# A gated recurrence feeding a two-layer block on one core: log sums, transposes and totals on 64-row tiles, and a longer list of steps

## The chip, the cores and the metric

The kernel runs on one core of one Trainium2 chip. The metric is the device time of one launch in microseconds, lower is better. The median of three runs before the change is 605.38 us (605.31 to 607.55).

## The reference

Two stages are chained. The first is a gated linear recurrence over 768 positions, for 4 batches and 8 heads of width 48; the second applies two weight matrices with an activation between them to the resulting 3072 rows of 384.

```python
f = 1.0 / (1.0 + np.exp(-f_logit))
for t in range(S):
    state = f[:, :, t, :, None] * state + einsum('bhd,bhe->bhde', k[:, :, t], v[:, :, t])
    y[:, :, t] = einsum('bhd,bhde->bhe', q[:, :, t], state)
x = y.transpose(0, 2, 1, 3).reshape(B * S, H * D)      # (3072, 384)
h = x @ w_in                                           # (3072, 2048)
sp = np.maximum(h, 0.0) + np.log1p(np.exp(-np.abs(h)))
out = (h * erf(sp)) @ w_out                            # (3072, 384)
```

All tensors of the recurrence are float32. The two weight matrices arrive as 8-byte numbers, which the kernel itself turns into float32 (a "rounding" of seven steps for each of 16 pieces, one step on ACT and six on VectorE).

## The kernel before

The rows are cut into 24 chunks of 128 positions, and each chunk into two halves of 64. A block is two chunks (256 rows), so there are 12 blocks.

For each chunk g the recurrence does the following; the short names are those of the list of steps.

- f, q, k, v: loads on SP's queue. `load_f` (L229) brings the gate logits as one DMA of 192 KB into `lt`, with the positions on the partitions. cl, ex, ln: clamp, exp and log of `lt`, for -log of the gate.
- d, `log_sums` (L396): running sums of the logs within each half, as one product of a 128x128 triangular matrix `tri` with `lt`, 384 columns, into one PSUM bank. e, `decays` (L400, L401): two exps out of that bank, into `dp` and `kd`. qd, kd (L414, L421): q and k times them, on VectorE.
- tq, tk, `transposes` (L437): four transposes of 128x128 each for q and for k into PSUM; aq, ak (L443, L449 or L451): copies of them to SBUF, on ACT or VectorE.
- ds, `state_products` (L499), and sc, `scores` (L510): products on 64x64 tiles into the two banks of `sc_all`. m and s: masks on the scores (L535 to L544). to, ta, `sum_totals` (L518): for chunks below 6 the total decay of each half, taken out of `dp` by products with columns of the identity; tt sends the totals of later chunks by small DMAs.
- st, `add_state` (L473 to L476), and sp, `copy_state` (L481): the running state of VectorE and its copies into `sv` on POOL (GpSimd), two per half chunk. v with four digits, L249, and w, L256: values into `sv`, by ACT copies in the first three chunks and by four small DMAs each later.
- y, `x_rows` (L580): the output rows, on 128x32 tiles; x, `copy_x` (L591): their copy to `xT` on ACT.

For each block the second stage does: h (L671), `hps`, 48 products of 256 columns with `w_in`, into two-bank tiles of `ps_moe`; c (L683) the copy to SBUF; ae to am the activation of a group of four row tiles on ACT and VectorE (L157, L160, L165, L625, L628); then the product with `w_out`. For blocks 0 and 1 that is `project_first` (L771, 384 columns). From block 2 on it is `project` (L822), seven products of half size instead of eight, which needs sums of blocks of the activations and of `w_out` (L709) and combines the results (L830, L838).

A float32 product runs as two TensorE records, a transpose as one.

[...]`ps_sc` holds two (`sc_all`), `ps_moe` two tiles of two banks, and `ps_at` two tiles of one bank each, handed round among log sums, the two sets of transposes and y (for the first chunks partly `ps_moe` is used instead).

The order of all instructions is written out. Every engine runs its own in that order. There are two parts. `EARLY` is a list of tokens that `early()` carries out one after another: it covers the start, the recurrence up to chunk 8's transposes and the hidden products of blocks 0 to 2. Filler products (z, `keep_busy`, L380) stand in it where TensorE has nothing to do. Behind it a loop over turns `it` = 2 to 11 emits one product per slot (`slots`) and at given slots the stages of two later chunks (`at`), activation steps, sums, loads and, through `weights_step` and `load_more`, the pieces of `w_out` that the list has not loaded and rounded. In turns 2 and 3 the products are those of `hidden(3)`, `project_first(0)`, `project_first(1)` and `hidden(4)`. From turn 4 on they are `project(it - 2)` and `hidden(it + 1)`, and in the last turn three `project` calls.

In this text a "visit" is a run of TensorE records on smaller tiles than 128x128 between records on the full array.

Of the kernel before, what the change touches and what calls it, by code (L numbers as in the profile page):

```python
# [33 lines left out]

# [40 lines left out]
def kernel(  # L75
# [46 lines left out]

    def heads(src, b, c):
        return src[b, :, c * P : (c + 1) * P, :].rearrange("h t d -> t h d")
# [53 lines left out]
    ps_at = main.enter_context(tc.tile_pool(name="ps_at", bufs=2, space=PSUM))  # L178
# [40 lines left out]
    FIRST, TOTALS = 3, 6  # L219


    lts = {}

    def load_f(g):
        b, c = divmod(g, NCH)
        blk, j = divmod(g, CPB)
        if blk not in lts:
            lts[blk] = lpool.tile([P, CPB, d_model], FP32, name="lt", tag="lt")
        nc.sync.dma_start(  # L229
            out=lts[blk][:, j, :].rearrange("t (h d) -> t h d", d=D), in_=heads(f_logit, b, c)  # L230
        )
# [12 lines left out]
    def half(c):  # L244
        return slice(C * c, C * (c + 1))

    def copy_sv(g, r, c):
        pairs = vts[g % NV][half(c)].rearrange("t (a r d) -> t a r d", r=2, d=D)
        nc.scalar.copy(out=svs[g % NSV][half(1 - r), r, c, :, PAD : PAD + D], in_=pairs[:, :, r, :])  # L249
# [133 lines left out]

    def pair_tile():
# [5 lines left out]
    def log_sums(g):  # L390
# [3 lines left out]
        else:  # L394
            dTs[g] = ps_at.tile([P, 512], FP32, name="ps_d", tag="at")[:, 0:d_model]
        nc.tensor.matmul(dTs[g], lhsT=tri[:], rhs=lts[blk][:, j, :], start=True, stop=True)  # L396

    def decays(g):
        ps = dTs.pop(g).rearrange("t (h d) -> t h d", d=D)
        nc.scalar.activation(out=dps[g % 2][:, :, 0:D], in_=ps, func=AF.Exp, scale=-1.0)  # L400
        nc.scalar.activation(out=kds[g % 2][:, :, 0:D], in_=ps, func=AF.Exp)  # L401
# [11 lines left out]
    def times_q(g):  # L413
        nc.vector.tensor_tensor(  # L414
# [4 lines left out]
    def times_k(g):  # L419
        kd = kds[g % 2][:, :, 0:D]  # L420
        nc.vector.tensor_tensor(  # L421
# [9 lines left out]

    def transposes(g, n):
        src = qd if n == "q" else kds[g % 2]
        tps[g, n] = ps_at.tile([P, HP, P], FP32, name="ps_t", tag="at")
        flat = src[:].rearrange("t (a r) d -> t a (r d)", r=2)
        for a in range(HP):
            nc.tensor.transpose(tps[g, n][:, a, :], flat[:, a, :], ident[:])  # L437

    def copy_q(g):
        qAs[g] = work.tile([P, 2, HP, P], FP32, name="qA", tag="qA")  # L440
        ps = tps.pop((g, "q"))
        for r in range(2):
            nc.scalar.copy(out=qAs[g][half(r), r], in_=ps[half(r)])  # L443

    def copy_k(g):
        kTs[g] = work1.tile([P, HP, P], FP32, name="kT", tag="kT")
        ps = tps.pop((g, "k"))
        if g < 9:
            nc.scalar.copy(out=kTs[g][:], in_=ps[:])  # L449
        else:  # L450
            nc.vector.tensor_copy(out=kTs[g][:], in_=ps[:])  # L451

    def stage_t(g):
# [3 lines left out]
        transposes(g, "k")  # L457
# [7 lines left out]
    totals = sc_all[:, 0, HP * (C + D) : HP * (C + D) + 2 * HP]  # L465
# [12 lines left out]
    def copy_state(k):  # L478
        g1, c1 = divmod(k + 1, 2)
        for r in range(2):  # L480
            nc.gpsimd.tensor_copy(  # L481
                out=svs[g1 % NSV][rows(r), r, c1, :, PAD : PAD + D], in_=state[rows(r)]
            )
# [31 lines left out]
    def sum_totals(g):  # L515
        pairs = dps[g % 2][:].rearrange("t (a r) d -> t a (r d)", r=2)
        for a in range(HP):
            nc.tensor.matmul(  # L518
                totals[:, 2 * a : 2 * a + 2], lhsT=pairs[:, a, :], rhs=ident[:, C - 1 : P : C],
                start=True, stop=True,  # L520
            )

    def copy_totals(g):
        nc.vector.tensor_copy(
            out=Tall[:, g].rearrange("p c a -> p a c"),
            in_=totals.rearrange("p (a c) -> p a c", c=2),
        )
# [36 lines left out]
    def x_rows(g, c):  # L564
        if c == 0:
            yts[g] = (
                pair_tile()[:, 0, 0 : n_k * P].rearrange("t (k n) -> t k n", k=n_k) if g < 2
                else ps_at.tile([P, n_k, P], FP32, name="y", tag="at")
# [17 lines left out]
    def copy_x(g):  # L586
        blk, j = divmod(g, CPB)
        if j == 0:
            xTs[blk] = work.tile([P, n_k, TB], FP32, name="xT", tag="xT")
        qAs.pop(g)  # L590
        nc.scalar.copy(out=xTs[blk][:, :, j * P : (j + 1) * P], in_=yts.pop(g)[:])  # L591
# [135 lines left out]
    def sum_h(gr):  # L727
# [4 lines left out]
        sums = next(sum_places)  # L732
# [27 lines left out]
    def project_first(blk):  # L760
# [563 lines left out]
```

## Time and profile before

| What | Value |
|---|---|
| Median of three runs | 605.38 us |
| Profiled execution, its own time | 610.34 us |
| Its span | 608.6 us |
| First hps product | 34.80 us |
| First product of L822 (turn 4 begins) | 226.99 us |
| hps, L671: records, mean length | 1152, 383 ns |
| log sums, L396: records, mean length | 48, 493 ns |
| transposes, L437: records of q and of k | 96 and 96 |
| filler, L380: records, busy | 72, 12.0 us |

The profile describes one execution. [...]records of one kind overlap; what one costs is the distance between the starts of two that follow each other. In a timeline row, the first number is the start, the second the time to the end of the merged group, and a bracket names the idle time before it and what ended it. "PEclk" is the granted clock of TensorE.

### The profile page before, as it was taken

Reading aid. Unit: us, or ns where it says so; the run is one execution under the profiler, and the core shown is the slowest. Engines: PE = TensorE matmul, PEld = TensorE weight load, DVE = VectorE, ACT = ScalarE, POOL = GpSimd, SP = SyncE. Lnnn points to the kernel's source line nnn. Section 1 sums busy time; section 2 is a strip of 40 time slices with the busy share of each in tenths; the row PEclk is TensorE's granted clock in tenths of the full one; section 3 lists DMA queues with packets and bytes.
Section 4 is the critical chain, followed back from the end, with each engine's and each line's share of the span. In section 5 each row is a group of like instructions: output and inputs, shape, how many; then the busy total and the mean of one; then the engine's idle time right before and its main releaser. Section 6 shows DMA issues by size and latency. Waiting matters only on the chain.

```text
span 608.6 us, 13919 instructions
## 1 busy us (share of the span) xinstructions
PE 590.3 (97%) x5769; PEld 517.1 (85%) x5769; DVE 430.2 (71%) x705; ACT 382.8 (63%) x483; POOL 92.3 (15%) x119
## 2 busy tenths in 40 slices
PE   8999999998899999999999999999999899999995
PEld 7788888886566789889989889989989789989995
DVE  4789889976975876867776677767686575648451
ACT  6738859787836687757757766857676446366000
POOL 1330342120404010220021200112011200000000
PEclk9999999999899999999999999999999999999998
DMA  9799966206130430520421421412310000000000
GB/s 187 211 234 238 236 146 128 32 2 156 32 74 2 99 59 1 105 53 3 89 57 14 79 57 24 80 41 40 54 41 1 2 26 1 27 1 2 27 26 30
DMA packets 152148, 41.34 MB, mean 68 GB/s; under 512 B 143888, under 2 KB 146960, under 8 KB 152080
## 3 DMA queue, kind: packets, MB, share of 16 engines
q1 hardware_dynamic: 149856, 39.81, 29.9%
q8 instruction: 47, 0.77, 0.5%
q10 hardware_dynamic: 2224, 0.59, 0.4%
q14 instruction: 21, 0.17, 0.1%
HBM read 35.59 MB, written 4.72 MB: 66 GB/s over the span
## 4 chain that ended last, share of the span: by engine, by line
PE 82%; DVE 6%; ACT 6%; DMA 2%; issue 1%; POOL 1%; SPq 1%; ACTq 0%; DVEq 0%; POOLq 0%
PE hps L671 36%; PE ops L822 25%; PE ops L771 6%; PE y L580 3%; PE ps_t L437 3%; PE ps_d L396 2%; PE sc L510 2%; PE sc L499 2%; PE busy L380 1%; ACT x L160 1%; DMA w_out_sb<-in_moe_w_out_dram 1%; DVE e L165 1%; POOL sv L481 1%; DVE qA L537 1%; DVE Hg L628 1%
## 5 line engine op out<-in xcount | busy, mean ns | idle before, releaser
L671 PE MATMUL hps<-xT,w_in_sb 128*128 128x256 f32 x1152 | 259.7, 383 | 2.4 <-ACT Hg L683 1.7
L671 PEld LDWEIGHTS hps<-xT,w_in_sb 128*128 128x128 f32 x1152 | 217.6, 191 | 34.5 <-ACT Hg L683 2.1
L165 DVE SCALAR_TENSOR_TENSOR e<-x,e 128x1024 f32<-128x1024 f32 x96 | 117.4, 1223 | 15.7 <-ACT x L160 15.3
L481 POOL COPY sv<-state 48x192 f32<-48x192 f32 x88 | 75.8, 861 | 340.7 <-DVE state L476 245.6
L160 ACT ACTIVATE x<-Hg,serf_bias 128x1024 f32<-128x1024 f32 x88 | 97.5, 1141 | 0.2
L157 ACT ACTIVATE e<-Hg 128x1024 f32<-128x1024 f32 x44 | 46.5, 1058 | 57.3 <-DVE Hg L628 57.1
L822 PE MATMUL ops<-wT,Hg 128*128 128x192 f32 x320 | 78.5, 329 | 0.0
L683 ACT COPY Hg<-hps 128x1024 f32<-128x1024 f32 x44 | 44.4, 1010 | 42.7 <-PE hps L671 42.5
L628 DVE TENSOR_TENSOR Hg<-Hg,e 128x1024 f32<-128x1024 f32 x44 | 53.7, 1221 | 24.5 <-ACT e L625 24.4
L822 PE MATMUL ops<-wT,scratch 128*128 128x192 f32 x288 | 67.9, 327 | 0.9 <-DVE scratch L830 0.9
L822 PE MATMUL ops<-w_out_sb,Hg 128*128 128x192 f32 x320 | 65.1, 326 | 0.0
L822 PEld LDWEIGHTS ops<-wT,Hg 128*128 128x128 f32 x320 | 55.8, 190 | 1.9
L822 PEld LDWEIGHTS ops<-w_out_sb,Hg 128*128 128x128 f32 x320 | 54.6, 190 | 2.0
L537 DVE TENSOR_TENSOR qA<-sc,tri 64x256 f32<-64x256 f32 x68 | 28.7, 422 | 35.7 <-PE sc L510 31.6
L625 ACT ACTIVATE e<-e 128x1024 f32<-128x1024 f32 x48 | 50.4, 1051 | 2.9 <-DVE e L165 2.8
L822 PEld LDWEIGHTS ops<-wT,scratch 128*128 128x128 f32 x288 | 50.3, 190 | 1.1 <-issue 1.1
L830 DVE TENSOR_TENSOR scratch<-scratch,ops 128x384 f32<-128x384 f32 (+1 forms) x40 | 19.9, 497 | 34.1 <-ACT scratch L838 26.6
L443 ACT COPY qA<-ps_t 64x512 f32<-64x512 f32 x48 | 27.8, 578 | 13.1 <-PE ps_t L437 12.7
L414 DVE TENSOR_TENSOR qd<-qn,dp 128x384 f32<-128x384 f32 x24 | 13.9, 579 | 28.6 <-ACT dp L400 28.6
L822 PE MATMUL ops<-w_out_sb,scratch 128*128 128x192 f32 x132 | 32.3, 326 | 0.0
L580 PEld LDWEIGHTS y<-qA,sv 128*32 128x32 f32 x1408 | 21.2, 110 | 8.7 <-issue 5.4
L838 ACT COPY scratch<-ops 128x192 f32<-128x192 f32 x10 | 3.2, 318 | 39.2 <-PE ops L822 39.2
(123 smaller groups left out, 692.6 us busy)
## 6 DMA issues: line engine op xcount, KB each, us to landing
lt<-in_f_logit_dram SPq DMA_DIRECT2D x24, 192.0 KB, 3.8
qn<-in_q_dram SPq DMA_DIRECT2D x24, 192.0 KB, 3.9
kn<-in_k_dram SPq DMA_DIRECT2D x23, 192.0 KB, 3.5
vt<-in_v_dram SPq DMA_DIRECT2D x23, 192.0 KB, 4.0
out_dram<-scratch SPq DMA_DIRECT2D x11, 384.0 KB, 2.6
sv<-in_v_dram SPq DMA_DIRECT2D x84, 48.0 KB, 2.9
w_out_sb<-in_moe_w_in_dram SPq DMA_DIRECT2D x4, 768.0 KB, 7.3
Hg<-in_moe_w_in_dram SPq DMA_DIRECT2D x4, 768.0 KB, 6.4
```

The lines of the kernel that those rows point to most:

```text
L157: nc.scalar.activation(out=dst[:], in_=h, func=AF.Exp)
L160: nc.scalar.activation(out=dst[:], in_=h, func=AF.Tanh, bias=serf_bias[:, i : i + 1], scale=SERF_KAB[i][0])
L165: nc.vector.scalar_tensor_tensor(out=e[:], in0=x[:], scalar=SERF_KAB[i][2], in1=e[:], op0=ALU.add, op1=ALU.mult)
L481: nc.gpsimd.tensor_copy(out=svs[g1 % NSV][rows(r), r, c1, :, PAD : PAD + D], in_=state[rows(r)])
L537: nc.vector.tensor_tensor(out=to, in0=sc[half(c), r], in1=tri1[half(c)].unsqueeze(1).broadcast_to((C, HP, C)), op=ALU.mult,)
L580: nc.tensor.matmul(y[M * i : M * (i + 1), kt, half(c)], lhsT=sv[:, r, c, a, o : o + M], rhs=qA[:, r, a, half(c)], start=(c == 0 and n == 0 ...
L625: nc.scalar.activation(out=e[0][:], in_=e[0][:], func=AF.Tanh, scale=SERF_C)
L628: nc.vector.tensor_tensor(out=h, in0=h, in1=e[0][:], op=ALU.mult)
L671: nc.tensor.matmul(hts[blk, gi][:, j, :], lhsT=w_in_sb[:, kt, ft * P : (ft + 1) * P], rhs=xTs[blk][:, kt, :], start=(kt == 0), stop=(kt == ...
L683: nc.scalar.copy(out=gr["h"], in_=hts.pop((blk, gi))[:])
L771: nc.tensor.matmul(ops[:, tt, 0:d_model], lhsT=gr["h"][:, j, tt * P : (tt + 1) * P], rhs=w_out_sb[:, ft, :], start=(ft == 0), stop=(ft == ...
L822: nc.tensor.matmul(place[n], lhsT=x[:, j, :], rhs=y, start=(gi == 0 and j == 0 and n in first), stop=(gi == n_g - 1 and j == 1), skip_grou ...
```

## The change

It has four parts.

1. From chunk 4 on (`SPLIT`), the log sums of a chunk are four products of 64x64 tiles with `tri1`, of 192 columns each. Their input has another layout: the partitions hold the two halves of the heads and the columns the two halves of the positions, so `load_f` issues four DMAs of 48 KB in place of one of 192 KB. The results lie in two PSUM banks, one for each half of the heads. From chunk 4 on the transposes are sixteen of 64x128 (one half of the positions each) in place of eight of 128x128, alternating between two banks. The totals are products of 64-row halves in all six chunks that have them.
2. `ps_at` becomes one tile of two banks, in place of two tiles of one bank. Log sums, the transposes of q and k together, and y take it in turn.
3. `EARLY` is another list and reaches further, to the masks of chunk 12's scores. It holds what turns 2 and 3 of the loop did: hidden products of blocks 3 and 4, `project_tile` (o) for blocks 0 and 1 in pieces of four products, the sums (sw, sh) and all loads and roundings of the weights. The loop begins with turn 4. Its slots from there on are as before, and `weights_step` and `load_more` are gone.
4. A token may name an engine (a, v or g for ACT, VectorE and POOL) for copies of values, of states and of x and for the copy of the transposed k. In the list nine of the twelve value copies go from ACT to POOL, and of the state copies two go to other engines before the first hps product, and three a little later. There are 31 filler products in place of 36, and the fills of the padding move into the list (`in`). ACT loads activation tables twice more.

The core of the diff:

```diff
-    ps_at = main.enter_context(tc.tile_pool(name="ps_at", bufs=2, space=PSUM))
+    ps_at = main.enter_context(tc.tile_pool(name="ps_at", bufs=1, space=PSUM))
...
-    FIRST, TOTALS = 3, 6
+    FIRST, SPLIT = 3, 4
...
+        lt = lts[blk][:, j, :]
+        if g < SPLIT:
+            nc.sync.dma_start(out=lt.rearrange("t (h d) -> t h d", d=D), in_=heads(f_logit, b, c))
+            return
+        w = d_model // 2
+        for n in range(2):
+            for u in range(2):
+                t0 = c * P + u * C
+                nc.sync.dma_start(
+                    out=lt[half(n), w * u : w * (u + 1)].rearrange("t (h d) -> t h d", d=D),
+                    in_=f_logit[b, HP * n : HP * (n + 1), t0 : t0 + C, :].rearrange("h t d -> t h d"),
+                )
...
+    def bank_pair(name):
+        return ps_at.tile([P, 2, 512], FP32, name=name, tag="at")
...
-        nc.tensor.matmul(dTs[g], lhsT=tri[:], rhs=lts[blk][:, j, :], start=True, stop=True)
+        w = d_model // 2
+        dTs[g] = banks[:, :, 0:w]
+        for i in range(2):
+            for c in range(2):
+                n = (c + i) % 2
+                nc.tensor.matmul(
+                    dTs[g][half(c), n, :], lhsT=tri1[half(n), :],
+                    rhs=lts[blk][half(n), j, w * c : w * (c + 1)], start=True, stop=True,
+                )
...
-        tps[g, n] = ps_at.tile([P, HP, P], FP32, name="ps_t", tag="at")
-        flat = src[:].rearrange("t (a r) d -> t a (r d)", r=2)
-        for a in range(HP):
-            nc.tensor.transpose(tps[g, n][:, a, :], flat[:, a, :], ident[:])
+        for i, src in enumerate((qd, kds[g % 2])):
+            for a in range(HP):
+                for c in range(2):
+                    o = (HP * i + a) * C
+                    nc.tensor.transpose(
+                        tps[g][:, c, o : o + C], pairs(src)[half(c), a, :], ident[half(c), half(c)]
+                    )
...
         for a in range(HP):
-            nc.tensor.matmul(
-                totals[:, 2 * a : 2 * a + 2], lhsT=pairs[:, a, :], rhs=ident[:, C - 1 : P : C],
-                start=True, stop=True,
-            )
+            for c in range(2):
+                nc.tensor.matmul(
+                    totals[:, c, a : a + 1], lhsT=pairs(dps[g % 2])[half(c), a, :],
+                    rhs=ident[half(c), C * (c + 1) - 1 : C * (c + 1)], start=True, stop=True,
+                )
...
-    def copy_state(k):
+    def copy_state(k, engine=nc.gpsimd):
...
+    def project_tile(blk, gi, tt):
+        if (gi, tt) == (0, 0):
+            ots[blk] = ps_moe.tile([P, 2, 512], FP32, name="ops", tag="moe")
+        gr = groups[blk, gi]
+        for j in range(FG):
+            ft = gi * FG + j
+            nc.tensor.matmul(
+                ots[blk][:, tt, 0:d_model], lhsT=gr["h"][:, j, tt * P : (tt + 1) * P],
+                rhs=w_out_sb[:, ft, :], start=(ft == 0), stop=(ft == n_ft - 1),
+            )
...
-        for it in range(2, n_blocks):
+        for it in range(ADJACENT - 1, n_blocks):
```

The list's passage around the first pieces of block 0's projection, before and after (o, h and c are projection, hidden products and their copies; r a rounding step; d to aq the recurrence of chunk 6):

```diff
-        c0_3 q9 au0_0 sp12 p8 ln8 st13 ah0_0 y5_0 r11_1 y5_1 ax0_1 am0_0 tk6 sp13 v9 h1_7 x5 at0_1 p10 ak6
+        ax1_1 au1_0 h2_6 at1_1 ah1_0 aw1_1 am1_0 c2_1 h2_7 au1_1 r10_0 r11_6 ah1_1 r10_1 d6 am1_1
+        c2_3 o0_0_0 e6 r10_2 r12_0 tt6 kd6 qd6 ae1_3 ds6 r12_1 tq6 r12_2 r13_0 o0_0_1 r12_3 aq6
```

## The prediction

> **What bounds the kernel now.** I read the page first, then the table of stretches, then TensorE's waits and timeline.
>
> ```profile
> span 608.6 us, 13919 instructions
> ...
> PE 590.3 (97%) x5769; PEld 517.1 (85%) x5769; DVE 430.2 (71%) x705; ACT 382.8 (63%) x483; POOL 92.3 (15%) x119
> ...
> PEclk9999999999899999999999999999999999999998
> ```
>
> TensorE is occupied for 97% of the span, no other engine above 71%. But busy is not useful: the groups hold 12.0 us of filler ("busy<-tri", x72), and rows are long. The stretches tell more:
>
> ```profile
> core 0: us, PE busy (x) PEld busy (x) DVE busy (x) ACT busy (x) POOL busy (x), PEclk, DMA share, GB/s
> 0.00:40.00 40.00, 36.18 (x670) 30.53 (x671) 26.52 (x63) 26.35 (x53) 12.11 (x28) 1.00 0.91 208
> 40.00:140.00 100.00, 98.96 (x1046) 83.08 (x1045) 88.74 (x125) 77.36 (x109) 25.54 (x32) 1.00 0.56 132
> 140.00:160.00 20.00, 15.93 (x118) 10.94 (x117) 14.19 (x19) 15.41 (x22) 2.32 (x3) 0.92 0.59 139
> 160.00:227.00 67.00, 67.00 (x598) 47.28 (x597) 50.59 (x81) 43.10 (x49) 14.59 (x13) 1.00 0.26 52
> 227.00:480.00 253.00, 252.96 (x2633) 232.67 (x2632) 180.35 (x303) 173.12 (x202) 34.24 (x45) 1.00 0.24 45
> ```
>
> From 227 to 480 us TensorE has no hole at all: there only fewer or cheaper TensorE records help. Holes are in the first 40 us and at 140 to 160. The latter's, in TensorE's timeline:
>
> ```profile
> 142.46 0.70 PE L671 MATMUL hps<-xT,w_in_sb 128*128 128x256 f32 x2 [1.65 <-ACT Hg L683]
> ...
> 149.79 4.14 PE L771 MATMUL ops<-w_out_sb,wT 128*128 128x384 f32 x12
> 156.29 0.66 PE L437 MATMUL ps_t<-ident,qd 128*128 128x128 f32 x4 [2.36 <-DVE qd L414]
> ```
>
> What a visit to small tiles costs, from the same view in the steady part:
>
> ```profile
> 305.02 0.60 PE L437 MATMUL ps_t<-ident,qd 128*128 128x128 f32 x4
> 305.46 0.60 PE L437 MATMUL ps_t<-ident,kd 128*128 128x128 f32 x4
> 305.90 6.21 PE L671 MATMUL hps<-xT,w_in_sb 128*128 128x256 f32 x28
> 312.04 1.10 PE L580 MATMUL y<-qA,sv 128*32 128x64 f32 x64
> 313.07 0.57 PE L499 MATMUL sc<-vt,kd 64*48 64x48 f32 x32
> 313.46 0.66 PE L510 MATMUL sc<-qA,kT 48*64 48x64 f32 x32
> 314.05 2.21 PE L671 MATMUL hps<-xT,w_in_sb 128*128 128x256 f32 x9
> ```
>
> The 28 hps records end at 312.11, so the last started at 311.73: 216 ns apart. The first y record then starts 0.31 after that one, 0.09 late. On leaving, the last sc record starts at 313.90 and hps at 314.05, 0.15 later where its four-tile step is 0.06: 0.09 to 0.11 lost. The nine hps records after it take 0.10 more than 8 steps of 216. So entering and leaving costs 0.09 + 0.02 (slower first step) + 0.11 + 0.10 = about 0.33 us. Inside, the 64x64 blocks run 32 records in 0.4 to 0.6 us, four abreast. Transposes need 109 ns per record and no switch.
>
> [...]
>
> **The change part by part.** Against the profiled execution: span 608.55, its own time 610.34; the median of the runs is 605.38, so I subtract the same microseconds from the median.
>
> *Log sums, 20 chunks.* Removed: 2 records of 384 columns, 323 ns apart, 0.65 us. Added: four products of 192 columns, 8 records, on four separate 64x64 tiles. The trace's 192-column record costs 162 ns; four abreast make two steps, 0.33, plus one visit, 0.33: 0.66. Net +0.01. Without concurrency it were 1.30 + 0.33; the sc rows with the same tiles exclude that. Free of the switch it saves 0.32.
>
> *Transposes, 20 chunks.* Removed 8 x 109 = 0.87. Added 16 transposes of 64 columns on 64x128 tiles, a form that this trace lacks. Two abreast, 8 steps of about 0.06 (64 columns stream in 0.056[...]): 0.48 + 0.33 = 0.81, net -0.06. One after another: 16 x 0.06 + 0.33 = 1.3, net +0.42, in all +8.4. Free of switching -0.39. I take two abreast. Both parts together -0.05 x 20 = -1.0 us. The bounds without any switch cost are -0.71 x 20 = -14.
>
> *Totals, six early chunks.* 16 records on pairs for 8; their 112 ns is a load of 128 columns, so 8 pairs cost what 8 loads did: 0 (bound +0.9 a chunk, beside waits of the first 80 us).
>
> *One tile of two banks instead of two one-bank tiles.* New waits: the next log sums after the copy of x, y after both transpose copies (it needs those anyway). In the steady part the copy of x ends at 313.71 and the next ps_d starts at 320.74; the smallest distance that I find from 227 us on is some 3 us. Cost 0; queued behind a late one would be all hps records. In the list, where log sums of chunks 5 and 4 stand 12 hps records (2.6 us) apart with an exp of 1.06 and two decays of 0.49 between, a miss costs under 1 us each: I allow +0.7.
>
> *SP's queue.* The log-gate load becomes four DMAs. A 48 KB issue took about 0.67 us on SP (four sv loads 2.7), the single load 0.4 to 0.8, so +2 us of queue per chunk. SP is issuing almost without a break from 41 to 74 us; five such loads stand there, so weight pieces behind them may start up to 10 us later. The rounding is ahead of its use by about that much, so 0 for the forecast, up to +4.
>
> *The list.* It now reaches the first product of L822, at 226.99 us. Adding what TensorE must do until there, record counts by the spacings above: hps 480 x 0.216 = 103.7, L771 128 x 0.323 = 41.3, log sums 8.4, transposes 11.3, y 12.4, sc 12.7, totals 5.4, and 29 visits' outer part 5.7: 201. So 26 us are lost: some 14.5 before the first hps at 34.80, 5.6 in the dip (1.65 + 2.36 + 8% of 20 us of clock), the rest in small waits. The dip's cause: the last two w_out pieces are issued at 140.22 and rounded on ACT and VectorE (L316, L318 onwards) just where chunk 9's qd is due; ACT sits 2.4 and VectorE 5.5 us before them. In the new list projection steps of block 0 stand among hps of block 2, and VectorE's work stands earlier: summing durations in list order, where TensorE has 95 us of stream VectorE has 93 (before 88), at 150 it has 143 (before 136). With VectorE some 10 us ahead at the start, its work is done when asked for. I take 4.5 of the 5.6 as recovered. What is late next is the last two pieces again, with hps of block 3 as cover.
>
> In the first 35 us two state copies go from POOL (median 0.55 us per half in this stretch, up to 1.5) to VectorE or ACT (0.35) and nine of twelve value copies from ACT to POOL. ACT is busy 26 of 40 us, and TensorE's waits there, mostly covered by the filler, end with qA, sv and x: -1.0 (bounds -4, if these chains set the start, and +3, if the piece now loaded earlier delays chunks 2 and 3). Other small waits: -0.5. Two more table loads, 1.28 each, lie in ACT's idle time. About 7.7 us of activation work (2 exp, 4 terms, 1 tanh) moves behind 227, where ACT is idle for 80 of 253 us: 0.
>
> The holes at 483 (1.6, POOL's sv) and 568 (1.0) lie in loops that stay: 0. Sum: -1.0 + 0.7 - 4.5 - 1.0 - 0.5 = -6.3: span 602.3, median 599.1, say 599.
>
> **The rivals.** *A, more gained:* the switch is mostly hidden or the start shortens by its bound; -6.3 - 8 = 591. For it: many new visits in the list stand next to other 64x64 work and share one. Against: 22 of the added visits in the loops stand alone among hps or ops. *B, slower:* the 64-row transposes go one after another. Place: after every stage of transposes; price 0.42 instead of -0.06, so 20 x 0.48 = +9.6: 608.7. It decides from about 0.3 us extra per chunk, where the list's gain is eaten. For it: no such tile in the trace, and 128 columns to load twice. Against: 64x64 tiles, which also pair row halves, run abreast. *C, the list gives its gain back:* SP's queue (+4) and readers of the single tile (+2) open holes as large as those that close: -6.3 + 6 = about 0, so 605, or 603 to 608. For it: SP's full queue to 74 us and log sums of two chunks 2.6 us apart. Against: after 75 us SP has gaps of 5 to 20 us.
>
> **How the numbers follow.** Forecast 0.50, A 0.13, B 0.20, C 0.17. I count a change within 0.5% (602.4 to 608.4) as none, about what a measurement of this kernel can tell. Forecast and A are faster (0.62, and a little of C: 0.64); C is mostly same, B's lower half too: 0.18; slower 0.18. The range reaches from A to B: 591 to 609.5; the forecast's own is 594 to 603.
>
> **What would show it.** Log sums: 8 records in about 0.35 us and the next hps 0.1 late. Transposes: pairs starting within 10 ns, 16 in about 0.5 us; a step of 0.06 for each single one would be B. The first L822 product near 221 instead of 227, no PEclk dip near 150, TensorE waiting under 1 us for qd. From there to the end 381.6 us as now, within 1.5. I am wrong if new holes of several us appear before it with SP or ps_at readers as releasers, or if the first hps comes later than 35 us.

## The result, and the profile after

No change that can be measured: the changed kernel takes 606.82 us (median of 12 runs, 604.03 to 609.21), the kernel before 606.26 us (12 runs, 605.15 to 609.11). The ratio is 1.0001 [0.998, 1.0023]. In the code of the changed kernel `log_sums` is L416 and L424, `transposes` L473 and L479, the scores' product L556, `sum_totals` L564, the hidden product L714 and `project` L861, with its combining steps at L869.

The page of the profile after, its first lines and the clock row:

```profile
span 602.6 us, 14596 instructions
...
PE 585.7 (97%) x6087; PEld 505.1 (84%) x6087; DVE 430.1 (71%) x707; ACT 385.8 (64%) x484; POOL 90.8 (15%) x118
...
PEclk9999999999999999999999999999999999999898
```

Against the page before this looks like a gain of 6.0 us (602.6 for 608.6). It is none. The execution profiled before took 610.34 us, longer than each of its 12 timed runs; the one profiled after took 604.03 us, the shortest of its 12. Two single executions are compared there, and each kernel spreads over 4 to 5 us. So the traces show where time moves, and only the medians what it comes to.

The table of stretches of the profile after (length, then busy time of each engine with its instructions, granted clock of TensorE, DMA):

```profile
core 0: us, PE busy (x) PEld busy (x) DVE busy (x) ACT busy (x) POOL busy (x), PEclk, DMA share, GB/s
0.00:40.00 40.00, 34.38 (x682) 29.13 (x686) 26.88 (x64) 24.69 (x49) 10.98 (x28) 0.96 0.83 186
...
140.00:160.00 20.00, 20.00 (x295) 12.26 (x294) 19.37 (x29) 17.94 (x27) 6.84 (x9) 1.00 0.38 63
160.00:227.00 67.00, 67.00 (x699) 53.98 (x698) 38.38 (x70) 39.15 (x49) 14.83 (x14) 1.00 0.39 75
...
480.00:500.00 20.00, 20.00 (x99) 17.96 (x98) 12.32 (x20) 13.09 (x14) 0.00 (x0) 1.00 0.02 5
500.00:602.60 102.60, 92.67 (x529) 89.57 (x528) 56.78 (x96) 37.06 (x40) 0.00 (x0) 0.96 0.05 17
```

The dip at 140 to 160 us is gone: TensorE is busy for 20.00 of 20 us, where it was 15.93. The first product of `project` starts at 220.73 us for 226.99. Two new things stand at the ends. The clock is 0.96 in the first 40 us, where it was 1.00: a window of 3.4 us at half clock, from 28.8 us. From 500 us on it is 0.96 too, and TensorE has no record for 10 us. Of these, 6.7 us lie behind its last record, with no work that half a clock could slow down; the profile before has the same 6.7. TensorE's waits name the hole that is new:

```profile
PE ops L861 <- DVE scratch L869: 3.3, 1, 3.3
...
PE sc L564 <- issue: 0.7, 1, 0.7
```

The columns are the total, the number of waits and the longest. The 3.3 us lie at 558.5 to 561.8 us. "issue" in the second row means that the trace shows nothing that TensorE waited for; it comes up again below.

The wait for a value of POOL at 481 to 483 us, which the prediction left in place, is gone. Both profiles of the kernel before have it (1.6 us; the first and e1 below), and none of the changed kernel has (the first, e2 and e13). In the profile before, a second half-clock window stood behind it, which the prediction did not read (clock 0.91; columns as above):

```profile
480.00:500.00 20.00, 18.30 (x136) 15.54 (x136) 13.62 (x23) 10.68 (x11) 3.44 (x2) 0.91 0.06 21
```

The timeline of all engines around the late hole, the rows that matter:

```profile
557.89 1.22 DVE L171 SCALAR_TENSOR_TENSOR e<-x,e 128x1024 f32<-128x1024 f32 x1
558.03 0.49 PE L861 MATMUL ops<-wT,scratch 128*128 128x192 f32 x2
...
559.14 1.06 ACT L668 ACTIVATE e<-e 128x1024 f32<-128x1024 f32 x1 [4.38 <-DVE e L171]
559.48 0.42 DVE L752 TENSOR_TENSOR scratch<-Hg,scratch 128x256 f32<-128x256 f32 x1
559.82 0.41 DVE L752 TENSOR_TENSOR Hg<-Hg 128x256 f32<-128x256 f32 x1
560.15 1.52 DVE L869 TENSOR_TENSOR scratch<-scratch,ops 128x384 f32<-128x384 f32 x3
561.82 0.98 PE L861 MATMUL ops<-wT,scratch 128*128 128x192 f32 x2 [3.30 <-DVE scratch L869]
```

TensorE stops at 558.5 us, since its next product needs a PSUM tile that L869 has still to read. VectorE comes to L869 only at 560.15, because an activation step (L171) and sums of the activation (L752) stand before it in its order. ACT has stood idle for 4.38 us, waiting for L171. So this looks like activation work that comes late on VectorE, not like a want of engine time; e5 and e10 test it. The first product behind the hole takes 0.98 us where it took 0.49: the clock was halved from 561.3 us, for 3.4 us.

Many executions can be read this way, since each comes with a span and a mean granted clock. As an estimate, their product is what the execution would take at full clock, and the rest of the span is what the clock took. Medians (a slow run of e8, 677.0 us at a mean clock of 0.849, is left out of its split below):

| | at full clock, us | lost by the clock, us | mean clock |
|---|---|---|---|
| before (67 runs) | 602.5 | 3.0 | 0.995 |
| changed kernel (12 runs) | 597.8 | 7.9 | 0.987 |
| changed kernel again, e2 (14 runs) | 598.1 | 8.5 | 0.986 |
| and once more, e13 (13 runs) | 597.9 | 7.9 | 0.987 |

By this split the new list does save some 4.5 us, and loses 5 us through TensorE's clock. That is the answer to where the gain went; the experiments ask what takes it.

The split is good for differences, less so for its columns. In the profiles before and after the clock is recorded at half behind TensorE's last record, from 604.0 of 608.6 us and from 598.8 of 602.6, with nothing there to slow down; that makes 2.3 and 1.9 us of the middle column. The clock's record also begins only 6.7 and 4.9 us after the start, and before that the filler runs at half speed (its records start 0.21 us apart, later 0.11). And the device time is longer than the span: by 1.7 us for the kernel before, by 1.4 for the changed one, but by 2.8 for each variant with a catch-up below (medians). No run shows why. To compare such a variant with the changed kernel, add 1.4 us to its time at full clock.

### The profile page after: what moved, and what is told of

Same layout as the page of the kernel before. It is cut to its first block, busy times and chain, and to the rows that moved or that the text cites. A ratio compares the mean times of both kernels' runs of the same rounds, so it can differ in the third digit from the quotient of the medians.

```text
span 602.6 us, 14596 instructions
## 1 busy us (share of the span) xinstructions
PE 585.7 (97%) x6087; PEld 505.1 (84%) x6087; DVE 430.1 (71%) x707; ACT 385.8 (64%) x484; POOL 90.8 (15%) x118
## 4 chain that ended last, share of the span: by engine, by line
PE 90%; DVE 4%; ACT 3%; issue 1%; POOL 0%; ACTq 0%; DVEq 0%; POOLq 0%
PE hps L714 41%; PE ops L861 27%; PE ops L814 7%; PE y L623 4%; PE ps_t L479 2%; PE sc L556 2%; PE sc L545 2%; PE ps_d L424 2%; PE busy L395 1%; DVE Hg L671 1%; PE ps_t L473 1%; PE sc L564 1%; ACT x L166 1%; ACT qA L491 1%; DVE scratch L752 1%
## 5 line engine op out<-in xcount | busy, mean ns | idle before, releaser
L714 PE MATMUL hps<-xT,w_in_sb 128*128 128x256 f32 x1152 | 258.5, 382 | 1.0 <-ACT xT L127 0.6
L714 PEld LDWEIGHTS hps<-xT,w_in_sb 128*128 128x128 f32 x1152 | 216.2, 190 | 32.7 <-issue 1.6
L171 DVE SCALAR_TENSOR_TENSOR e<-x,e 128x1024 f32<-128x1024 f32 x96 | 117.3, 1223 | 14.1 <-ACT x L166 13.4
L127 POOL COPY sv<-state 48x192 f32<-48x192 f32 x78 | 71.0, 911 | 309.7 <-DVE state L524 261.9
L861 PE MATMUL ops<-wT,Hg 128*128 128x192 f32 x320 | 80.3, 335 | 0.0
L861 PE MATMUL ops<-wT,scratch 128*128 128x192 f32 x288 | 68.3, 329 | 3.3 <-DVE scratch L869 3.3
L861 PE MATMUL ops<-w_out_sb,Hg 128*128 128x192 f32 x320 | 65.8, 329 | 0.0
L861 PEld LDWEIGHTS ops<-wT,Hg 128*128 128x128 f32 x320 | 55.9, 192 | 2.4 <-issue 1.4
L861 PEld LDWEIGHTS ops<-w_out_sb,Hg 128*128 128x128 f32 x320 | 54.0, 190 | 2.1 <-issue 1.7
L861 PEld LDWEIGHTS ops<-wT,scratch 128*128 128x128 f32 x288 | 50.7, 192 | 3.6 <-issue 3.6
L869 DVE TENSOR_TENSOR scratch<-scratch,ops 128x384 f32<-128x384 f32 (+1 forms) x40 | 19.9, 497 | 33.5 <-ACT scratch L877 26.9
L861 PE MATMUL ops<-w_out_sb,scratch 128*128 128x192 f32 x132 | 32.6, 330 | 0.0
L623 PE MATMUL y<-qA,sv 128*32 128x64 f32 x1408 | 25.1, 222 | 0.2 <-POOL qA L587 0.2
```

What stands on the lines that cost most here:

```text
L127: (engine.copy if engine is nc.scalar else engine.tensor_copy)(out=out, in_=in_)
L171: nc.vector.scalar_tensor_tensor(out=e[:], in0=x[:], scalar=SERF_KAB[i][2], in1=e[:], op0=ALU.add, op1=ALU.mult)
L623: nc.tensor.matmul(y[M * i : M * (i + 1), kt, half(c)], lhsT=sv[:, r, c, a, o : o + M], rhs=qA[:, r, a, half(c)], start=(c == 0 and n == 0 ...
L714: nc.tensor.matmul(hts[blk, gi][:, j, :], lhsT=w_in_sb[:, kt, ft * P : (ft + 1) * P], rhs=xTs[blk][:, kt, :], start=(kt == 0), stop=(kt == ...
L861: nc.tensor.matmul(place[n], lhsT=x[:, j, :], rhs=y, start=(gi == 0 and j == 0 and n in first), stop=(gi == n_g - 1 and j == 1), skip_grou ...
```

## The experiments

The theory after the result: the tile shapes are neutral, the list wins 4 to 5 us, and two causes take them back, a backlog of activation work that the loop carries to its end, and a sparser start (less filler, new waits) in which the clock falls. Rivals: the shapes cost what the list gains; the runs drift and hide a gain; missing filler alone explains the clock. All ratios are to the kernel before, measured beside the variant on the same chip, with a 95% interval. e1 to e4 ran on one chip, e5 to e8, e9 to e11 and e12 to e14 on three others.

**The kernel before and the changed one again.** No edit.

> The kernel before, once more. The medians are equal (606.26 and 606.82) although the two profiles differ by 6 us in the span (608.6 and 602.6). Theory 1: the profile of before showed an ordinary execution, and the new kernel loses its gain in ordinary executions to more half-clock windows (3.4 us each, 1.7 us lost each): then this profile again begins L822 at 227 +- 1 us, with the hole at 140 to 160, and its executions have a mean clock of about 0.990. Theory 2: the profile of before was a slow one: then this profile begins L822 near 223 and has a span near 605, with the hole smaller or gone.

> The changed kernel, once more, on the same chip. Both theories: L822 begins at 220.7 +- 1 us plus 1.7 us for each half-clock window before it. Theory 1: more half-clock windows than in the kernel before of the same call, mean clock 0.983 to 0.988, and the span is the one of 602.6 plus 1.7 for each window more. Theory 2: as many windows as before, ratio 1.00.

Measured: 607.33 us, ratio 0.999 [0.9972, 1.0008], and 608.16 us, ratio 1.0005 [0.9987, 1.0023]. The changed kernel is no faster on another chip either. The second profile of the kernel before, its table of stretches and TensorE's waits:

```profile
core 0: us, PE busy (x) PEld busy (x) DVE busy (x) ACT busy (x) POOL busy (x), PEclk, DMA share, GB/s
...
140.00:160.00 20.00, 15.92 (x121) 10.90 (x122) 14.79 (x20) 14.86 (x21) 2.20 (x3) 1.00 0.57 139
```

```profile
PE ps_t L437 <- DVE qd L414: 2.4, 1, 2.4
...
PE ops L822 <- DVE scratch L830: 0.9, 1, 0.9
```

The holes of the dip are there again (15.92 for 15.93 us busy), but the clock in it is 1.00, not 0.92. The holes stand in both profiles of the kernel before, the half-clock window behind them in the first alone. In the same way the window behind the wait for POOL at 483 us stands in the first (0.91 at 480 to 500 us), not here (1.00). The late wait at L822, the counterpart of L861, is 0.9 us.

The second profile of the changed kernel, its ends:

```profile
core 0: us, PE busy (x) PEld busy (x) DVE busy (x) ACT busy (x) POOL busy (x), PEclk, DMA share, GB/s
0.00:50.00 50.00, 42.49 (x711) 36.17 (x712) 33.70 (x75) 27.53 (x54) 10.75 (x28) 0.90 0.86 203
...
550.00:606.90 56.90, 46.62 (x276) 46.06 (x274) 27.45 (x56) 8.85 (x11) 0.00 (x0) 0.94 0.07 22
```

The clock is 0.90 in the first 50 us here and 0.97 in the first profile of the same kernel; the first product of `project` came at 224.42 us instead of 220.73. So the start's loss varies between executions of one kernel, from one window of 3.4 us to three, and to four in e13 below (0.86): 1.5, 5 and 7 us lost of 50, at 1.7 a window. Of the 3.4 us that the clock takes from 550 us on, one window of 3.4 us behind the hole makes 1.7; the rest, as an estimate from the first profile (1.9 us there), lies behind TensorE's last record.

**The list without the 64-row log sums and transposes.**

```diff
-    FIRST, SPLIT = 3, 4
+    FIRST, SPLIT = 3, 24
...
+        transposes(g, "k")
```

(The second line stands in the step tq and in the loop's stage of transposes, so that every chunk has q and k done on the full array; the gate logits then come by one DMA again. The totals keep the changed form.)

> The new list with log sums and transposes on the full array (one DMA per gate load, two transposes' sets of eight records), totals as in the change. From the profile of the change a visit for log sums costs 0.68 us against 0.65, one for transposes 0.84 against 0.88: a sum of about 0 over 20 chunks. Theory 'the tiles are neutral': the same as the changed kernel within 1 us. Rival 'the tiles cost': 3 us or more faster, since SP issues 60 DMAs fewer and the array's shape changes some 80 times less.

Measured: 607.81 us, ratio 1.001 [0.9992, 1.0028]; at full clock 598.5 us against 598.1 of e2. The shapes are worth nothing either way, and the list alone has both the gain and the loss.

**More filler in the start**: twelve filler products more (43 in place of 31).

```diff
-r0_2 tk1
+r0_2 z3 tk1
...
-y1_1 kd3
+y1_1 z3 kd3
...
-r3_0 tq3
+r3_0 z3 tq3
...
-st4 tk3
+st4 z3 tk3
```

> The changed kernel with 12 filler products more, in four places of the first 35 us where TensorE waits for copies (before the transposes of k of chunks 1 and 3 and those of q of chunks 2 and 3). Theory 1: the half-clock window near 29 us goes, the mean clock rises by some 0.003 and the median falls by 1.5 to 3 us. Rival: the windows are not caused there; no change, or up to 1 us slower for the filler.

Measured: 606.49 us, ratio 0.998 [0.9965, 0.9994], with waits for ACT's `qA` of 0.3 us in place of 1.7. The loss by the clock falls from 8.5 to 5.4 us; at full clock the kernel is 1.6 us longer (599.7). Filler buys clock and costs time of its own: net 1.7 us against e2, measured beside it.

**Catch up the activation backlog in turn 4.** One more activation step in every nine slots of that turn.

```diff
-            step = s % 9 in (2, 6)
+            step = s % 9 in ((2, 4, 6) if it == ADJACENT - 1 else (2, 6))
```

> The changed kernel with three activation steps per nine slots in turn 4 in place of two, so that the 7.7 us of activation work which the new list leaves to the loop is caught up at once. Theory 'backlog': the hole of 3.47 us near 559 (ops waits for the combining on VectorE) shrinks to about 1 us as before, the half-clock window behind it goes, the end comes 3 to 5 us earlier than in the changed kernel: about 602.5 to 603.5, ratio 0.993. Rival 'the hole belongs to the slots of turn 11': it stays at 3.4 us, ratio 1.00.

Measured: 604.72 us, ratio 0.9974 [0.9948, 0.9999], against a kernel before of 606.7. TensorE's waits in its profile:

```profile
PE ps_d L424 <- ACT xT L127: 1.5, 1, 1.5
...
PE ops L861 <- DVE scratch L869: 0.9, 1, 0.9
PE hps L714 <- DVE scratch L869: 0.8, 1, 0.8
PE y L623 <- POOL sv L127: 0.6, 1, 0.6
```

The late hole shrinks from 3.3 to 0.9 us, as wide as before the change, and the window behind it is gone (from 563.1 us on two records take 0.49 us, as at full clock). So the hole comes from the backlog. But three new holes of 1.5, 0.8 and 0.6 us stand in turn 4 (at 243 to 263 us), because ACT and VectorE, now fuller there, bring the copies of x and the sums late. At full clock nothing is won (598.2 for 598.1 in e2, and 1.4 us more outside the span); what is won is the clock, 4.8 us lost for 8.5. Only the window behind the hole, 1.7 us of these 3.7, follows from the edit: the start is unchanged, and e10, which closes the hole too, still loses 6.0.

**Both**, e4 and e5 together.

> Both: the catching-up and the 12 filler products. Theory 'two separate leaks' (windows of half clock at the start, backlog at the end): gains add up, clock 0.993 or more, about 601 to 602.5, ratio 0.991. Rival 'only the end counts': as e5, within 0.7 us.

Measured: 604.68 us, ratio 0.9965 [0.9951, 0.9979]; 2.4 us lost by the clock, 599.5 at full clock. Beside e5 the filler takes 2.4 us off the clock's loss, nearly what it did in e4 (3.1), and takes its price again (1.3 us). In time the two come out even (604.68 for 604.72), which is what the rival forecast.

**Totals on the full array again.** They are a part of the change of their own, and in both profiles of the changed kernel TensorE stands still among them near 35 us with nothing shown that it waits for.

```diff
-            for c in range(2):
-                nc.tensor.matmul(totals[:, c, a : a + 1], lhsT=pairs(dps[g % 2])[half(c), a, :], ...)
+            nc.tensor.matmul(totals[:, 2 * a : 2 * a + 2], lhsT=pairs(dps[g % 2])[:, a, :],
+                rhs=ident[:, C - 1 : P : C], start=True, stop=True)
```

> The changed kernel with the totals of six chunks as four products on the full array (8 records) in place of eight on 64-row halves (16 records). In the profiles so far TensorE waits 0.7 to 2.2 us for nothing that is shown ('issue') in or just ahead of the totals of chunk 3, near 34 us. Theory 'the many short records of the totals let TensorE run dry and the clock drop': the 'issue' hole goes and a window of half clock with it, 1 to 3 us faster than the changed kernel. Rival 'the hole is not tied to the totals' form': it moves to the next block, the time stays within 1 us.

Measured: 604.83 us, ratio 0.9965 [0.9949, 0.9981]; 597.9 at full clock, 5.4 lost by the clock. Its profile has no such hole. That looked like a cause found, and did not stand: e8 and e11 below have the same form of totals, and TensorE stands still for 1.6 and 2.1 us at the same place. The gain by the clock is real as a median (its ratio and that of the changed kernel, though, come from different chips); the hole isn't explained by the form of the totals.

**All three**, e4, e5 and e7.

> Catching-up, filler and full-array totals. If all three leaks are separate: about 600 to 602, ratio 0.989. If the totals' form is no leak: as e6 within 0.7 us.

Measured: 604.63 us, ratio 0.9956 [0.9941, 0.9972]; 599.6 at full clock and 2.4 lost. No better than e6: beside the extra filler, the totals' form adds no gain that can be seen.

**The kernel before with less filler**, 28 products in place of 36.

```diff
-ex3 z4
+ex3 z1
...
-sp4 z7 ak3
+sp4 z3 ak3
...
-m3_01 z2 m3_10
+m3_01 z1 m3_10
```

> The kernel before with 28 filler products in place of 36: four becomes one, seven three and two one, in the stretch from 22 to 35 us. Theory 'fewer useful and filler records in the start let the clock drop': windows of half clock appear between 25 and 45 us, the mean clock falls from 0.995 to 0.990 or less, the time at full clock (span times clock) stays at 602 +- 1, the median rises by 2 to 3 us, ratio 1.004. Rival 'the new list's drops come from its order, not from missing filler': clock and time as before.

Measured: 607.3 us, ratio 1.0009 [0.9994, 1.0023]; clock 0.9925 for 0.997 of the kernel before beside it. The median points the way of the theory, 4.5 us lost instead of 1.8, a rise of 2.7 us where the changed kernel's is 5; but the kernel before lost 3.0 to 3.6 us on the other chips, and the ratio's interval includes 1. Inconclusive as to time. Less filler than the changed kernel has isn't enough to bring the old list to a clock of 0.987.

**The catch-up spread out**: one activation step more at two slots of each of turns 4 to 8.

```diff
-            step = s % 9 in (2, 6)
+            step = s % 9 in (2, 6) or it < 9 and s in (48, 100)
```

> The changed kernel with the backlog caught up by two activation steps more in each of turns 4 to 8, at slots 48 and 100, away from the stages. In e5 the catching-up in one turn closed the hole near 559 (3.47 to 1.03) but opened three in turn 4 (1.70, 0.93, 0.73). Expected: the late hole at 1 us, none of the three above 0.5: 2 to 3 us less at full clock than e5, median 602 to 603, ratio 0.994. Rival: the holes come with any added step; as e5.

Measured: 604.71 us, ratio 0.995 [0.9928, 0.9973]. TensorE's waits from 227 us on:

```profile
PE hps L714 <- DVE scratch L869: 1.0, 1, 1.0
PE ops L861 <- DVE scratch L869: 0.9, 1, 0.9
```

The late hole is closed to 0.9 us at the price of one of 1.0 us in turn 4, instead of three. At full clock its span is the shortest of all, 595.6 us (with the 1.4 us more outside the span, about 1 us better than the changed kernel); 6.0 us are still lost by the clock. In its profile the clock is 0.79 at 20 to 28 us and 0.96, 0.62 and 0.71 up to 32, 36 and 42: 5.1 us lost, three windows' worth; at 555 to 566 us, around the late wait, it is 1.00.

**The best of the parts**: e10, e4 and e7 together.

> Spread catching-up, the 12 filler products and the totals on the full array together: clock 0.996 as in e8, and 2 to 3 us less than e8 at full clock: median 601.5 to 603, ratio 0.992 or 0.993, the fastest so far. Rival: as e8, 604.6.

Measured: 602.0 us (6 runs, 601.48 to 603.62), ratio 0.9915 [0.9884, 0.9946]. It beats the kernel before by 4.4 us (602.0 for 606.39 beside it), and with it the changed kernel, whose own ratios lie between 0.9988 and 1.0005. Its page:

```profile
span 600.4 us, 14555 instructions
...
PEclk9999999999999999999999999999999999999999
```

and its waits:

```profile
PE sc L563 <- issue: 2.1, 1, 2.1
```

All slices of the clock row are nines, and this execution's mean clock is 0.998: 1.2 us lost, less than one window takes (1.7). In the median it is 597.0 us at full clock and 2.7 lost. The wait without a releaser is still there.

**Transposes of k ahead of the copy of q**, in the start. The changed kernel's new waits there are mostly one kind: the transposes of k of chunks 0, 1 and 3 wait for ACT's copy of the transposed q, since both now lie in one tile. e4's filler stands just at two of them, so filler and waits were not yet told apart.

```diff
-to0 aq0 tk0 ta0
+to0 tk0 aq0 ta0
...
-aq1 v2_01g r0_2 tk1 q3
+tk1 aq1 v2_01g r0_2 q3
...
-aq3 st4 tk3 m2_00
+tk3 aq3 st4 m2_00
```

> Edit: in the changed kernel's list, for chunks 0, 1 and 3, the transposes of k stand ahead of the copy of the transposed q instead of behind it. In the changed kernel both sets of transposes lie in one PSUM tile, and those of k wait for ACT's copy of q's three times in the start (0.28, 0.75 and 0.71 us in its second profile, 1.7 us in all, the last at 29.7 us where the first half-clock window begins); the kernel before, with two tiles, has none of these waits. Theory (the single tile's waits are part of what starves TensorE in the start, and so of the clock's fall): the three waits go, the first product of project comes 1 to 2 us earlier, the loss by the clock falls from about 8 us to 6 or less, the ratio is 0.997 or less. Rival 1 (the waits cost only themselves or nothing, the clock falls for another reason): the waits go, the loss by the clock stays within 1 us of that of e13, the time at full clock falls by at most 1.7 us, ratio 0.997 to 1.001. Rival 2 (the waits move: the copies of q now come later and scores or output rows wait instead): same time, new waits for qA of the same sum.

> No edit: the changed kernel in the same call as e12 and e14, as their yardstick. Expected as in its earlier runs: ratio 1.000 to 1.001, about 598 us at full clock, about 8 us lost by the clock, three waits of the transposes of k for the copy of q in the start with 1.5 to 1.7 us in all.

Measured: e12 608.02 us, ratio 1.002 [0.9997, 1.0043]; 599.4 at full clock, 6.7 lost. e13 607.39 us, ratio 0.9988 [0.9966, 1.001]; 597.9 and 7.9. TensorE's waits in e13:

```profile
PE ps_t L473 <- ACT qA L491: 1.7, 3, 0.7
```

and in e12:

```profile
PE sc L564 <- issue: 2.1, 1, 2.1
PE sc L556 <- ACT kT L127: 1.7, 2, 1.2
```

The three waits are gone and have come back as waits of the scores for ACT's copy of the transposed k, with the same sum: rival 2, but for the copy that is waited for. The chain transposes, copy of q, copy of k, scores runs through ACT whichever part waits. The clock takes 1.2 us less, less than the theory asked for, and the time at full clock is 1.5 us more. So these waits aren't by themselves what makes the clock fall. The stretch of e13's profile up to 50 us:

```profile
core 0: us, PE busy (x) PEld busy (x) DVE busy (x) ACT busy (x) POOL busy (x), PEclk, DMA share, GB/s
0.00:50.00 50.00, 43.88 (x708) 36.70 (x709) 33.86 (x75) 27.43 (x54) 11.30 (x28) 0.86 0.81 188
```

Busier than in e2, and at a lower clock; but a record lasts longer at half clock (the hps records from 39.2 us on 634 ns, where they take 379 at full clock), so the clock itself raises the busy time.

**The swap and the spread catch-up together**, e12 and e10.

> Edit: e12 and e10 together (transposes of k ahead of the copy of q, and one activation step more at two slots of each of turns 4 to 8; no more filler, totals as changed). Theory (the single tile's waits feed the clock's fall in the start): 6.0 us lost by the clock in e10 become 4 or less, ratio 0.991 to 0.993, as good as e11 without any filler more. Rival 1 (clock unaffected): ratio 0.993 to 0.996, 5 to 7 us lost by the clock.

Measured: 603.86 us, ratio 0.9947 [0.9934, 0.996]; 597.6 at full clock, 4.2 lost. By ratio it is e10 again (0.995), as rival 1 has it; the loss by the clock is near the theory's figure (4 or less), but the time at full clock is 2.0 us above e10's, so nothing is won. The swap doesn't replace the filler.

## Why the prediction was wrong

It forecast 599 us and faster; the kernel stayed where it was. Two terms that it put at nothing failed: the activation work left to the loop (4.1 us in the profiles) and what the clock takes in the start (one to four half-clock windows, 1.7 us lost in each, where the two profiles of the kernel before have none). By its steps:

- *Log sums and transposes, -1.0.* The mechanism was right, the size a little off. A visit for each, alone among L861 records, in TensorE's timeline of the profile after:

```profile
314.74 0.49 PE L861 MATMUL ops<-wT,scratch 128*128 128x192 f32 x2
315.16 0.56 PE L424 MATMUL ps_d<-lt,tri 64*64 64x192 f32 x8
315.64 0.92 PE L861 MATMUL ops<-w_out_sb,Hg 128*128 128x192 f32 x4
...
323.22 0.49 PE L861 MATMUL ops<-w_out_sb,scratch 128*128 128x192 f32 x2
323.64 0.46 PE L479 MATMUL ps_t<-ident,qd 64*128 64x64 f32 x8
323.94 0.41 PE L479 MATMUL ps_t<-ident,kd 64*128 64x64 f32 x8
324.28 0.59 PE L861 MATMUL ops<-wT,Hg 128*128 128x192 f32 x2
```

  The log sums start 0.09 us after the place where the next 162-ns step would stand and hold the array for 0.49 us, and the first record after them takes 0.10 more: 0.68 us, where two full records took 0.65. The transposes start 0.09 late, hold 0.64 and cost 0.10 behind: 0.84 us, where eight took 0.88. Together nothing, as e3 confirms. Rival B falls: in the records of the profile after the two transposes of a pair start 0 to 5 ns apart, and the pairs follow at about 63 ns. The 0.33 us for entering and leaving, taken from other visits of the trace before, was the term that decided this, and it held.
- *One PSUM tile, +0.7.* The mechanism was right, its place and size wrong. It was looked for between log sums of chunks 5 and 4; it stands before the first hidden product, where k's transposes wait for the copy of q three times (1.5 to 1.7 us) and q's for the copy of k once (0.4): about 2 us. The kernel before has none of these waits.
- *Totals, 0.* Right at full clock (e7 597.9 us, e2 598.1); in the median e7 lost less by the clock, 5.4 us for 8.5, on another chip.
- *SP's queue, 0.* Right as far as the waits show: the largest waits for a load's work before 90 us are 0.4 us each, for the rounding of `w_in` and for the logs of `lt`.
- *The dip, -4.5.* Right as to the holes. Wrong in that it counted 1.6 us of clock as lost in every execution (about 1.3 of the 4.5): of the two profiles of the kernel before, the first has it (0.92), e1 doesn't (1.00).
- *The start, -1.0, and small waits, -0.5.* Wrong: the first hidden product comes at 36.2 us in the first profile, 39.1 and 39.2 in e2 and e13, not at 34.8; later than 35 us was one of its signs of being wrong. The sum had no term for what fewer filler products and a sparser TensorE do to the clock there. The filler cut from 36 to 31 was mentioned in the description of the change and priced at nothing by silence.
- *"The first L822 product near 221".* 220.73 in the first profile, but 224.42 and 224.87 in e2 and e13, which have three and four half-clock windows before it. The gain of 6.3 us before turn 4 was met in the first pair of profiles, each with one window there: luck of these two executions.
- *"About 7.7 us of activation work ... moves behind 227, where ACT is idle for 80 of 253 us: 0", and the holes in the loops that stay, 0.* This is the step that failed. ACT has the time, but the work isn't bound by ACT's time: it goes step by step through ACT and VectorE in a written order, at two steps in nine slots, so that a backlog at turn 4 is a backlog at the last turn. There it opens 3.3 us where 0.9 us stood, and a half-clock window of 1.7 us behind it, 4.1 us in all. e5 and e10 show it by catching up. The other hole that was to stay, at 483 us, went.
- *"The rest 381.6 us as now, within 1.5"* held in number (602.6 - 220.73 = 381.9), by cancelling: the second profile of the kernel before needs 604.2 - 226.03 = 378.2 us from the same point, so the rest grew by 3.7. The late hole is 2.4 more (3.3 for 0.9), the window 1.7, and the time after the last TensorE record 1.8 (6.7 for 4.9); against these the wait for POOL at 483 us is gone, about 1.6. These come to 4.3, so 0.6 the other way has no name. The first profile of the kernel before had a window and a long end of its own, which is why the number held against it.
- *Subtracting from the median.* The sum was made against a profile slower than every timed run, so losses that the median didn't have were counted as recoverable.

Without clock terms the forecast's sum is about -5, and at full clock -4.7 was measured (597.8 for 602.5). That they agree is luck in part: up to turn 4 the list wins more (226.03 us in e1; 220.73 less one window in the changed kernel's first profile, 7.0 us), the wait for POOL is gone, and the late hole takes 2.4 back. The clock then took what was left. Rival C, "the list gives its gain back", named what happened, at the time measured, but by SP's queue, which did nothing, and the single tile, which is 2 us of it at most. A slip in its chances, 0.62 for 0.50 and 0.13, changes nothing.

On the clock, the traces show this. In the profile before, the half-clock windows begin at 156.87 and 484.55 us, in the one after at 28.80 and 561.28; each lasts 3.41 us, and the starts lie 96 and 156 steps of 3.413 us apart. Counted back to the start, these steps begin 3.27 us behind the first instruction in the one profile and 1.50 us in the other. The loss varies between executions: 12 of the changed kernel have mean clocks of 0.983 to 0.991, 67 of the kernel before, beside e1 to e4, 0.986 to 1.000. By the split the clock takes 7.9 of 605.7 us from the changed kernel, 1.3%, or some 6 us without the stretch behind the last record.

Idle time alone doesn't tell where the clock falls. In the 3.41 us ahead of the four windows TensorE was busy for 31% and 50% of the time in the profile before, for 84% and 19% in the one after, and ahead of those that begin at about 20.6, 30.8 and 37.7 us in e13 for 66 to 79%. In the profile before it was busy for 52% from 139.80 to 143.21 us, and the full clock followed.

The work in the records tells more. As an estimate, count each TensorE record's columns at 0.84 ns (216 ns for the 256 columns of an hps record), times the share of the 128x128 array that its tile covers. The prediction's row of 64 y records on 128x32 tiles, 64 columns each, is 1.10 us long and 0.86 us of such work. Cut the profiles before and after into these steps of 3.413 us, from the clock's first record to TensorE's last. Of the 343 steps that are not at half clock themselves, four have less than 0.30 of their time in such work (0.22 and 0.29 before, 0.29 and 0.14 after), and half a clock follows each; the others have 0.34 or more, and it follows none. The 0.14 is the late hole. In the start of the profile after, transposes, small tiles and waits leave 0.29 at 25.4 us, with half a clock behind it, and 0.34 at 32.2 us, without. So as an estimate a little filler, or the place where the steps begin, can decide how many windows fall. This describes two profiles; no run was made to test it.

Two things stay open. Which part of the new list thins out the start isn't settled: more filler lowers the loss (5.4 us for 8.5, e4), but e9 does not show that less filler is enough, and in e12 the clock's loss hardly falls when the waits for ACT move. And no run tells what TensorE waits for near 35 us.

## What to carry to other kernels

When a step list reaches further and leaves work to the loop behind it, ask not whether the engine has idle time but at what rate the loop works a backlog off; if it never does, price it where the loop ends. A gain of less than 1% has to be larger than what TensorE's clock can take (here 7.9 of 605.7 us): read spans and mean clocks of many executions, split each into time at full clock and time lost, and see what lies outside the span. Take no hole's clock from one profile as recoverable until a second profile has it too. Where TensorE works on small tiles, judge a stretch by the work in it rather than by the busy time; that is the estimate from two profiles above.

## What was not expected of the hardware

- A single wait of 3.3 us in an otherwise full stretch was followed by a half-clock window of 3.4 us in all three profiles of the changed kernel (from 561.3, 565.5 and 566.7 us); the waits of 0.6 to 1.5 us in e5's turn 4 were followed by none (1.00 at 240 to 270 us). Behind the wait of 1.6 us for POOL the profile before has one (0.91), e1 none (1.00).
- The share of busy time doesn't tell where the clock will fall. In the first 50 us TensorE is busy for 43.88 us in e13 and 42.74 us in e11, and the clock is 0.86 and 1.00.
- In the profile before POOL took 3.86 us for the two state copies before 483 us; its 44 pairs of such copies took 0.74 to 6.67 us, 1.5 in the median. TensorE waited 1.61 us there for the second of them. In the profile after, the last two take 1.59 us and there is no wait. Why is not known.
- The time after the last TensorE record is 4.9 us in e1, 5.1 in e11 and 5.2 in e5, but 6.7 in the profiles before and after and in e4, and 7.0 in e2. Its cause was not looked into.
